# Linear attention beside a gated MLP: the key sum taken through DMAs and VectorE instead of one matmul, its den steps placed later, three loads joined

## The chip, the core and the metric

The program runs on one core of one Trainium2 chip. The metric is the device time of one execution in microseconds (us). The kernel before took 179.99 us (median of three runs, 179.78 to 180.3). Engines are named as in the profile: PE (TensorE), DVE (VectorE), ACT (ScalarE), POOL (GpSimd) and SP, which here only issues DMAs.

## What is computed

One input `x` (2048 tokens of 512 features, bfloat16) goes through two branches, mixed by a gate per token:

```python
phi = lambda t: jnp.where(t > 0, t + 1, jnp.exp(t)) + 1e-6
pq, pk = phi(q), phi(k)                     # q, k, v = x @ wqkv, 32 heads of 16
kv  = einsum("bhsd,bhse->bhde", pk, v)
z   = einsum("bhsd->bhd", pk)               # sum of phi(k) over all tokens
den = einsum("bhqd,bhd->bhq", pq, z)[..., None] + 1e-6
a   = (einsum("bhqd,bhde->bhqe", pq, kv) / den) merged @ wo
b   = (silu(x @ w1) * (x @ w3)) @ w2        # hidden width 1376
g   = sigmoid((x * gate_w).sum(-1))
out = g * a + (1 - g) * b
```

What the change touches is `z`: 512 sums over 2048 tokens, which every token's `den` needs, and so must be present in all 128 partitions.

## The kernel before, in words

Tokens are taken in 16 tiles of 128 (`t`), and in the second half in four blocks of 512 (`tb`). The order of the instructions on every engine is the order in which they are written in the program; each engine works through its own list in that order, and waits where an operand is not ready.

**First half.** Loads are issued on SP: `x` in natural layout (`xN`, L116 and L128), `x` transposed by DMA (`xT`, L110), and all weights (L113, L130 to L143). For each token tile PE projects q and k (L167); ACT takes the exponential and DVE the rest of phi (L180 to L185). PE accumulates `G = x^T phi(k)` in four PSUM banks (L215). POOL adds each tile of phi(k) into `zacc`, 128 partitions by 512 features (L195, L199); the last tile's sum is written as bfloat16 to `zaccb`. So `zaccb` still has to be summed over the 128 partitions.

**Between the halves.** One matmul of a matrix of ones by `zaccb` (L372) gives that sum in all partitions, and a DVE copy (L373) puts it in `zb`. Then `G` is copied out of PSUM to `Gsb` (L376 DVE, L378 ACT).

**Second half.** For block `tb`, `glu_step(tb, fc)` runs ten times (fc = 0..9): four matmuls with `w1` (L262), four with `w3` (L268), Silu on ACT (L273) and a product on DVE (L274) that writes `hT`. Both matmul groups use `mm_tile()`, four PSUM banks in turn: a group can start when the reader of the group four before it is done, and for the `w3` group that reader is the DVE product two chunks earlier. In block 0 other steps stand between the chunks: `den_step(0..3)` after chunks 0, 1, 3 and 6, `kv_step` after chunk 2 (L385, L389), `m2_step` after chunk 4 (L398 to L402), and `rem_step(0)` after chunk 7 (L229 to L252: the last 96 columns of the hidden width and the gate column, whose result is transposed by a DMA). `rem_step` takes two of the same four banks. Then four `out_step`s, one for each token tile: L410 multiplies `pqT` by `M2`, L423 multiplies `hT` by `w2`, L427 mixes them, L440 stores. The den steps of the next block are spread over them.

**A den step.** `den_products(t)` (POOL, L281) multiplies phi(q) of tile t by `zb` into `pr`; `den_sums(t)` (DVE) reduces it by head (L285), adds 1e-6 (L288) and takes the reciprocal (L292); `den_scale(t)` (POOL, L296) scales phi(q), and a transposing DMA on SP (L301) puts it into `pqT`, which L410 reads. `den_step(t)` issues the sums of t, the products of t + 1 and the scale of t, in that order; the products of tile 0 are issued once, ahead of the loop (L442).

Of the kernel before, what the change touches and what calls it, by code (L numbers as in the profile page):

```python
# [9 lines left out]
ALU = mybir.AluOpType  # L10
AX = mybir.AxisListType
FP32 = mybir.dt.float32
BF16 = mybir.dt.bfloat16
# [3 lines left out]
def kernel(  # L17
# [17 lines left out]
    nc = tc.nc  # L35
    P = nc.NUM_PARTITIONS

    Bb, S, D = A_x.shape
# [3 lines left out]
    KC = D // P  # L42
# [4 lines left out]
    FC = F // P  # L47
# [10 lines left out]
    w1_r = B_w1.rearrange("(kc d) f -> d kc f", d=P)  # L58
    w3_r = B_w3.rearrange("(kc d) f -> d kc f", d=P)

    consts = ctx.enter_context(tc.tile_pool(name="consts", bufs=1))
    work = ctx.enter_context(tc.tile_pool(name="work", bufs=2))
    psum = ctx.enter_context(tc.tile_pool(name="psum", bufs=1, space=bass.MemoryType.PSUM))
    ctx.enter_context(tc.manual_schedule())

    warm = nc.const_aps.tensor(1.0, [P, 256], BF16)
# [1 line left out]
    make_identity(nc, ident[:])  # L68


    ones = consts.tile([P, P], BF16, name="ones")
    nc.gpsimd.memset(ones[:], 1.0)
    bmask = consts.tile([P, HPC, Dh], BF16, name="bmask")
    nc.gpsimd.memset(bmask[:], 1.0)
    nc.gpsimd.affine_select(
        out=bmask[:], in_=bmask[:], pattern=[[-Dh, HPC], [0, Dh]], compare_op=ALU.is_ge,
# [3 lines left out]
        out=bmask[:], in_=bmask[:], pattern=[[Dh, HPC], [0, Dh]], compare_op=ALU.is_ge,  # L80
# [5 lines left out]
    zacc = consts.tile([P, D], FP32, name="zacc")  # L86
    zaccb = consts.tile([P, D], BF16, name="zaccb")
    zb = consts.tile([P, D], BF16, name="zb")

# [9 lines left out]
    w1 = consts.tile([P, KC, F0], BF16, name="w1")  # L101
    w3 = consts.tile([P, KC, F0], BF16, name="w3")
    w2 = consts.tile([P, FC + 1, D], BF16, name="w2")
    xT = consts.tile([P, KC, S], BF16, name="xT")
    act_pre = consts.tile([P, 1], BF16, name="act_pre")
    dq = nc.sync
# [5 lines left out]
    def load_wqk(kc):  # L112
        dq.dma_start(out=wqk[:, kc, :], in_=wqkv_r[:, kc, 0 : 2 * D])  # L113
# [6 lines left out]
    nc.scalar.dma_start(out=touch[:], in_=wqkv_r[:, 1:3, 0:16])  # L120
    for kc in range(KC):
        load_wqk(kc)
    natural = {3: (2, 4), 5: (4, 8), 7: (8, 12), 11: (12, 16)}
    for t in range(2, NT):
        load_xT(t)
        if t in natural:
# [2 lines left out]
    with nc.allow_non_contiguous_dma(reason="gate column"):  # L129
        dq.dma_start(  # L130
            out=wr[:, :, 2 * FR : NR], in_=gate_w.rearrange("(kc d o) -> d kc o", d=P, o=1)
        )
    dq.dma_start(out=wr[:, :, 0:FR], in_=w1_r[:, :, F0:F])
    dq.dma_start(out=wr[:, :, FR : 2 * FR], in_=w3_r[:, :, F0:F])
    for w, w_r, cuts in ((w1, w1_r, (0, KC)), (w3, w3_r, (0, 2, KC))):
        for a, b in zip(cuts, cuts[1:]):
            dq.dma_start(out=w[:, a:b, :], in_=w_r[:, a:b, 0:F0])
    dq.dma_start(out=wv[:], in_=wqkv_r[:, :, 2 * D : 3 * D])
    dq.dma_start(out=wo[:], in_=A_wo.rearrange("(kc d) n -> d kc n", d=P))
    w2_r = B_w2[0:F0, :].rearrange("(fc f) d -> f fc d", f=P)  # L140
    for a, b in ((0, 5), (5, FC)):
        dq.dma_start(out=w2[:, a:b, :], in_=w2_r[:, a:b, :])
    dq.dma_start(out=w2[:FR, FC, :], in_=B_w2[F0:F, :])  # L143

    pq = consts.tile([P, NT, D], BF16, name="pq")
# [11 lines left out]
    def mm_tile():  # L157
        turn["mm"] += 1
        return bank[4 + (turn["mm"] - 1) % 4]
# [53 lines left out]
    def g_step(t, kcs=range(KC)):  # L213
        for kc in kcs:
            nc.tensor.matmul(  # L215
                bank[kc][:], lhsT=xN[:, t, kc * P : (kc + 1) * P], rhs=pk[t][:],
                start=(t == 0), stop=(t == NT - 1),
            )


    def rem_step(tb):

        hr = hrem[tb % 2]
        for half in range(2):
            ps = mm_tile()[:].rearrange("p (j n) -> p j n", j=2)
            for j in range(2):
                t = tb * TPB + half * 2 + j
                for kc in range(KC):
                    nc.tensor.matmul(  # L229
                        ps[:, j, 0:NR], lhsT=xT[:, kc, t * P : (t + 1) * P],  # L230
                        rhs=wr[:, kc, 0:NR], start=(kc == 0), stop=(kc == KC - 1),
                    )
            t0 = tb * TPB + half * 2
            sg = work.tile([P, 2, FR], BF16, tag="sgr", name="sgr")
            nc.scalar.activation(out=sg[:], in_=ps[:, :, 0:FR], func=ACT.Silu)
            nc.scalar.activation(
                out=th_all[:, t0 : t0 + 2], in_=ps[:, :, 2 * FR], func=ACT.Tanh, scale=0.5
            )
            nc.vector.tensor_tensor(
                out=hr[:, half * 2 : half * 2 + 2, 0:FR], in0=ps[:, :, FR : 2 * FR],  # L240
                in1=sg[:], op=ALU.mult,
            )
        tl = slice(tb * TPB, (tb + 1) * TPB)
        nc.vector.tensor_scalar(
            out=g_all[:, tl], in0=th_all[:, tl], scalar1=0.5, scalar2=0.5,
            op0=ALU.mult, op1=ALU.add,
        )
        nc.vector.tensor_scalar(
            out=omg_all[:, tl], in0=th_all[:, tl], scalar1=-0.5, scalar2=0.5,
            op0=ALU.mult, op1=ALU.add,  # L250
        )
        dq.dma_start(  # L252
            out=hT[tb][:, FC, :].rearrange("p (tt q) -> p tt q", q=P),
            in_=hr[:].rearrange("p tt f -> p (tt f)"), transpose=True,
        )

    def glu_step(tb, fc):
        fs = slice(fc * P, (fc + 1) * P)
        tok = slice(tb * TB, (tb + 1) * TB)
        g_ps = mm_tile()  # L260
        for kc in range(KC):
            nc.tensor.matmul(  # L262
                g_ps[:], lhsT=w1[:, kc, fs], rhs=xT[:, kc, tok],
                start=(kc == 0), stop=(kc == KC - 1),
            )
        u_ps = mm_tile()
        for kc in range(KC):
            nc.tensor.matmul(  # L268
                u_ps[:], lhsT=w3[:, kc, fs], rhs=xT[:, kc, tok],
                start=(kc == 0), stop=(kc == KC - 1),  # L270
            )
        sg = work.tile([P, TB], BF16, tag="sg", bufs=3, name="sg")
        nc.scalar.activation(out=sg[:], in_=g_ps[:], func=ACT.Silu)  # L273
        nc.vector.tensor_tensor(out=hT[tb][:, fc, :], in0=u_ps[:], in1=sg[:], op=ALU.mult)  # L274
# [4 lines left out]
    def den_products(t):  # L279
        pr[t] = work.tile([P, D], FP32, tag="pr", bufs=3, name="pr")  # L280
        nc.gpsimd.tensor_tensor(out=pr[t][:], in0=pq[:, t, :], in1=zb[:], op=ALU.mult)  # L281
# [21 lines left out]
    def den_step(t):  # L303

        den_sums(t)
        if t + 1 < NT:
            den_products(t + 1)
        den_scale(t)
# [57 lines left out]
    for t in range(2, NT):  # L366
# [1 line left out]
        if t + 2 < NT:  # L368
            k_step(t + 2)
        g_step(t)  # L370
    z_ps = mm_tile()
    nc.tensor.matmul(z_ps[:], lhsT=ones[:], rhs=zaccb[:], start=True, stop=True)  # L372
    nc.vector.tensor_copy(out=zb[:], in_=z_ps[:])  # L373
    for kc in range(KC):
        if kc % 2 == 0:
            nc.vector.tensor_copy(out=Gsb[:, kc, :], in_=bank[kc][:])  # L376
# [3 lines left out]
    def kv_step():  # L380
        kv_ps = ab_tile()[:].rearrange("p (c q) -> p c q", q=P)
        for c in range(KC):
            cs = slice(c * P, (c + 1) * P)
            for kc in range(KC):
                nc.tensor.matmul(  # L385
                    kv_ps[:, c, :], lhsT=wv[:, kc, cs], rhs=Gsb[:, kc, cs],
                    start=(kc == 0), stop=(kc == KC - 1),
                )
        nc.vector.tensor_tensor(  # L389
            out=kvT[:], in0=kv_ps,  # L390
            in1=bmask[:].rearrange("p h d -> p (h d)")[:, None, :].to_broadcast([P, KC, P]),
            op=ALU.mult,
        )

    def m2_step():
        for c in range(KC):
            ps = ab_tile()
            nc.tensor.matmul(ps[:], lhsT=kvT[:, c, :], rhs=wo[:, c, :], start=True, stop=True)  # L398
            if c % 2 == 0:
                nc.scalar.activation(out=M2[:, c, :], in_=ps[:], func=ACT.Copy)  # L400
            else:
                nc.vector.tensor_copy(out=M2[:, c, :], in_=ps[:])  # L402
# [36 lines left out]
                cs = slice(2 * P, D)  # L439
            dq.dma_start(out=rows[:, cs], in_=o[:, cs])  # L440

    den_products(0)  # L442
    den_at = {0: 0, 1: 1, 3: 2, 6: 3}
    for tb in range(NTB):
        for fc in range(FC):
            glu_step(tb, fc)
            if tb == 0:
                if fc in den_at:
                    den_step(den_at[fc])
                if fc == 2:  # L450
                    kv_step()
                if fc == 4:
                    m2_step()
                if fc == 7:
                    rem_step(0)
        for tt in range(TPB):
            out_step(tb, tt)
            if tb + 1 < NTB:
                if tt == 0:
                    hT[tb + 1] = work.tile([P, FC + 1, TB], BF16, tag="hT", name="hT")  # L460
                if tt == 1:
                    rem_step(tb + 1)
                den_step((tb + 1) * TPB + tt)
# [30 lines left out]
```

## Time and profile before

| | |
|---|---|
| runs | 179.78, 179.99, 180.3 us |
| the profiled execution: its own time | 179.65 us |
| its span, first to last instruction | 177.8 us |
| PE busy | 174.2 us (98% of the span), 880 matmuls |
| DVE, ACT, POOL busy | 100.4, 62.3, 63.0 us |
| granted TensorE clock | 1.000 over the span |

The profile's page gives busy time by engine, groups of instructions by line, the DMA issues with their time to landing, and the chain of work that ended last. The timeline gives single instructions: start, duration, engine, line, tiles. A matmul of 128x512 is recorded with 379 ns, but four in a row take 0.86 us, since each starts before the one ahead of it has ended; the chain counts the pace, 0.216 us each.

### The profile page before, as it was taken

The numbers are of one execution on the slowest core, as the hardware profiler recorded it, in microseconds if no ns is written. First come the engines' busy times: TensorE is split into PE (matmuls) and PEld (weight loads), VectorE is DVE, ScalarE is ACT, GpSimd is POOL, SyncE is SP. The second block draws the span as 40 slices with busy tenths as digits, with TensorE's granted clock in tenths as the row PEclk, the third lists the DMA queues.
The fourth block names the chain that finished last, engine by engine and source line by source line (L and its number), as shares of the span: only waits on it lengthen the run. The fifth ranks groups of instructions, "written<-read, shape, count | busy, mean of one in ns | idle before, by whom it ended". The sixth has DMA issues, their size and how long they took to land.

```text
span 177.8 us, 2504 instructions
## 1 busy us (share of the span) xinstructions
PE 174.2 (98%) x880; PEld 84.1 (47%) x880; DVE 100.4 (56%) x194; ACT 62.3 (35%) x113; POOL 63.0 (35%) x105
## 2 busy tenths in 40 slices
PE   8999999999999999999999999999999999999993
PEld 5444444444454464644444464444445444444453
DVE  0299888888899662576344166634325564333222
ACT  3354544544735332331332223242321223342130
POOL 5086667656577340446300044540004432000000
PEclk9999999999999999999999999999999999999999
DMA  5989769994002111233100013520000342000001
GB/s 175 269 206 207 149 121 240 404 383 166 4 0 59 30 36 27 55 77 104 30 0 4 0 33 85 92 59 4 0 0 29 89 92 59 0 0 0 29 33 59
DMA packets 28940, 15.15 MB, mean 85 GB/s; under 512 B 20896, under 2 KB 27264, under 8 KB 28928
## 3 DMA queue, kind: packets, MB, share of 16 engines
q1 hardware_dynamic: 28656, 14.98, 31.9%
q8 instruction: 7, 0.11, 0.3%
q10 hardware_dynamic: 272, 0.01, 0.1%
q14 instruction: 5, 0.04, 0.1%
HBM read 8.43 MB, written 2.10 MB: 59 GB/s over the span
## 4 chain that ended last, share of the span: by engine, by line
PE 98%; DVE 0%; issue 0%
PE bank L423 21%; PE bank L262 19%; PE bank L268 19%; PE bank L167 16%; PE bank L215 8%; PE bank L410 8%; PE bank L229 3%; PE bank L315 2%; PE bank L385 1%; PE bank L398 0%; PE bank L322 0%; DVE o L427 0%; PE bank L372 0%
## 5 line engine op out<-in xcount | busy, mean ns | idle before, releaser
L274 DVE TENSOR_TENSOR hT<-bank,sg 128x512 bf16<-128x512 f32 x40 | 27.2, 680 | 30.9 <-PE bank L268 30.9
L268 PE MATMUL bank<-xT,w 128*128 128x512 bf16 x160 | 41.1, 379 | 0.0
L262 PE MATMUL bank<-xT,w 128*128 128x512 bf16 x160 | 41.1, 379 | 0.0
L423 PE MATMUL bank<-w,hT 128*128 128x512 bf16 (+3 forms) x198 | 40.7, 355 | 0.0
L273 ACT ACTIVATE sg<-bank 128x512 bf16<-128x512 f32 x40 | 23.9, 597 | 46.9 <-PE bank L262 46.9
L296 POOL TENSOR_TENSOR pqs<-pq,rden 128x512 bf16<-128x512 bf16 x16 | 16.9, 1055 | 65.0 <-issue 60.0
L167 PE MATMUL bank<-wqk,xT 128*128 128x512 bf16 x128 | 30.8, 383 | 0.0
L427 DVE SCALAR_TENSOR_TENSOR o<-bank,omg_all,aga 128x512 bf16<-128x512 f32 (+2 forms) x18 | 12.5, 692 | 28.1 <-PE bank L423 28.0
L423 PEld LDWEIGHTS <-hT 128*128 128x128 bf16 (+1 forms) x198 | 18.5, 98 | 19.8
L199 POOL TENSOR_TENSOR zacc<-zacc,pk 128x128 f32<-128x128 f32 x56 | 23.5, 449 | 10.8 <-DVE pk L185 10.8
L268 PEld LDWEIGHTS <-w 128*128 128x128 bf16 x160 | 15.7, 98 | 18.9
L262 PEld LDWEIGHTS <-w 128*128 128x128 bf16 x160 | 15.6, 98 | 18.4
L415 ACT ACTIVATE aga<-bank,g_all 128x512 f32<-128x512 f32 x16 | 11.0, 687 | 28.9 <-PE bank L410 28.9
L167 PEld LDWEIGHTS <-xT 128*128 128x128 bf16 x128 | 12.5, 99 | 15.5 <-issue 0.5
L281 POOL TENSOR_TENSOR pr<-pq,zb 128x512 f32<-128x512 bf16 x16 | 18.4, 1154 | 1.9 <-DVE zb L373 1.9
L215 PE MATMUL bank<-pk,xN 128*128 128x512 bf16 x64 | 16.5, 379 | 0.0
L410 PE MATMUL bank<-M,pqT 128*128 128x512 bf16 x64 | 16.4, 378 | 0.0
L180 ACT ACTIVATE eq<-bank 128x512 bf16<-128x512 f32 x16 | 9.4, 597 | 16.1 <-PE bank L167 16.1
L185 DVE SCALAR_TENSOR_TENSOR pk<-bank,emk 128x512 bf16<-128x512 f32 x16 | 11.1, 692 | 1.7
L180 ACT ACTIVATE ek<-bank 128x512 bf16<-128x512 f32 x16 | 9.4, 597 | 6.7 <-PE bank L167 6.7
L185 DVE SCALAR_TENSOR_TENSOR pq<-bank,emq 128x512 bf16<-128x512 f32 x16 | 11.1, 692 | 0.6
L285 DVE TENSOR_REDUCE den<-pr 128x32 f32<-128x512 f32 x16 | 10.8, 677 | 0.0
(47 smaller groups left out, 81.6 us busy)
## 6 DMA issues: line engine op xcount, KB each, us to landing
w<-in_B_w_dram SPq DMA_DIRECT2D x4, 640.0 KB, 9.6
out_dram<-o SPq DMA_DIRECT2D x15, 128.0 KB, 1.9
xN<-in_A_x_dram SPq DMA_DIRECT2D x3, 512.0 KB, 4.2
w<-in_B_w_dram SPq DMA_DIRECT2D x1, 1280.0 KB, 7.6
wqk<-in_A_wqkv_dram SPq DMA_DIRECT2D x4, 256.0 KB, 4.0
xN<-in_A_x_dram SPq DMA_DIRECT2D x2, 256.0 KB, 2.9
wv<-in_A_wqkv_dram SPq DMA_DIRECT2D x1, 512.0 KB, 10.8
wo<-in_A_wo_dram SPq DMA_DIRECT2D x1, 512.0 KB, 11.1
```

Source lines behind the costliest of these rows:

```text
L167: nc.tensor.matmul(ps[:], lhsT=xT[:, kc, t * P : (t + 1) * P], rhs=w[:, kc, :], start=(kc == 0), stop=(kc == KC - 1),)
L180: nc.scalar.activation(out=e[:], in_=ps[:], func=ACT.Exp)
L185: nc.vector.scalar_tensor_tensor(out=dst, in0=ps[:], scalar=0.0, in1=em[:], op0=ALU.max, op1=ALU.add)
L199: nc.gpsimd.tensor_tensor(out=(zaccb if t == NT - 1 else zacc)[:, cs], in0=zacc[:, cs], in1=pk[t][:, cs], op=ALU.add,)
L215: nc.tensor.matmul(bank[kc][:], lhsT=xN[:, t, kc * P : (kc + 1) * P], rhs=pk[t][:], start=(t == 0), stop=(t == NT - 1),)
L262: nc.tensor.matmul(g_ps[:], lhsT=w1[:, kc, fs], rhs=xT[:, kc, tok], start=(kc == 0), stop=(kc == KC - 1),)
L268: nc.tensor.matmul(u_ps[:], lhsT=w3[:, kc, fs], rhs=xT[:, kc, tok], start=(kc == 0), stop=(kc == KC - 1),)
L273: nc.scalar.activation(out=sg[:], in_=g_ps[:], func=ACT.Silu)
L274: nc.vector.tensor_tensor(out=hT[tb][:, fc, :], in0=u_ps[:], in1=sg[:], op=ALU.mult)
L281: nc.gpsimd.tensor_tensor(out=pr[t][:], in0=pq[:, t, :], in1=zb[:], op=ALU.mult)
L410: nc.tensor.matmul(a_ps[:], lhsT=pqT[:, c, ts], rhs=M2[:, c, :], start=(c == 0), stop=(c == KC - 1),)
L423: nc.tensor.matmul(b_ps[:, 0:w], lhsT=hT[tb][:n, fc, tl], rhs=w2[:n, fc, cs], start=(fc == 0), stop=(fc == FC),)
```

## The change

```diff
-    ones = consts.tile([P, P], BF16, name="ones")
-    nc.gpsimd.memset(ones[:], 1.0)
+    zaT = consts.tile([P, KC, P], BF16, name="zaT")
+    zTb = consts.tile([P, KC], BF16, name="zTb")
+    zrow = dram.tile([1, D], BF16, name="zrow")
...
-    natural = {3: (2, 4), 5: (4, 8), 7: (8, 12), 11: (12, 16)}
+    natural = {3: (2, 4), 5: (4, 8), 8: (8, 16)}
...
-    for w, w_r, cuts in ((w1, w1_r, (0, KC)), (w3, w3_r, (0, 2, KC))):
+    for w, w_r, cuts in ((w1, w1_r, (0, KC)), (w3, w3_r, (0, KC))):
...
-    for a, b in ((0, 5), (5, FC)):
-        dq.dma_start(out=w2[:, a:b, :], in_=w2_r[:, a:b, :])
+    dq.dma_start(out=w2[:, 0:FC, :], in_=w2_r)
...
-    z_ps = mm_tile()
-    nc.tensor.matmul(z_ps[:], lhsT=ones[:], rhs=zaccb[:], start=True, stop=True)
-    nc.vector.tensor_copy(out=zb[:], in_=z_ps[:])
+    dq.dma_start(out=zaT[:], in_=zaccb[:], transpose=True)
+
+    def z_step():
+        zT = work.tile([P, KC], FP32, tag="zT", bufs=1, name="zT")
+        nc.vector.tensor_reduce(out=zT[:], in_=zaT[:], op=ALU.add, axis=AX.X)
+        nc.vector.tensor_copy(out=zTb[:], in_=zT[:])
+        with nc.allow_non_contiguous_dma(reason="512 sums to one row"):
+            dq.dma_start(out=zrow[0, :].rearrange("(kc p) -> p kc", p=P), in_=zTb[:])
+        dq.dma_start(out=zb[:], in_=zrow[0:1, :].to_broadcast([P, D]))
...
-    den_products(0)
-    den_at = {0: 0, 1: 1, 3: 2, 6: 3}
+    den_at = {4: 0, 5: 1, 6: 2, 8: 3}
     for tb in range(NTB):
         for fc in range(FC):
             glu_step(tb, fc)
             if tb == 0:
+                if fc == 0:
+                    z_step()
+                    den_products(0)
                 if fc in den_at:
                     den_step(den_at[fc])
```

The sum over partitions is now made in five steps: a transposing DMA turns `zaccb` so that tokens lie along the free axis; DVE reduces each of the 512 rows to one number, and copies them to bfloat16; a DMA writes the 512 numbers as one row to a scratch tensor in DRAM; a second DMA reads that row into all 128 partitions of `zb`. The reduction, the copy and the last two DMAs are issued after chunk 0 of block 0, and `den_products(0)` after them. The den steps 0 to 3 move to after chunks 4, 5, 6 and 8. Three DMAs are added and three go, since three pairs of loads (`xN` tiles 8 to 15, `w3`, `w2`) become one DMA each; the two halves of `xN` are now issued together, after the transposing load of tile 8.

## The prediction

> **What bounds the kernel now.** I read four views, in this order. First the page's busy times and the chain that ended last: is one engine the whole time?
>
> ```profile
> PE 174.2 (98%) x880; PEld 84.1 (47%) x880; DVE 100.4 (56%) x194; ACT 62.3 (35%) x113; POOL 63.0 (35%) x105
> ...
> PE 98%; DVE 0%; issue 0%
> ```
>
> It is. TensorE's matmuls follow one another from 0.84 us to 175.07 us. Then the waits of PE alone, which hold one line:
>
> ```profile
> PE bank L315 <- PEq L478: 0.8, 1, 0.8
> ```
>
> PE waits only for the program's start. So nothing is gained by making another engine earlier; what counts is matmul work removed and waits of PE made new. Third, the chain in order of time, around the change:
>
> ```profile
> 45.89 0.86 PE bank L215 x4
> 46.75 0.22 PE bank L372
> 46.97 0.86 PE bank L262 x4
> ```
>
> The matmul that goes is 0.22 us of the chain (its pace of 0.216 us; the 379 ns of its row overlap its neighbour), with no gap on either side.
>
> Fourth, the timeline from 44 to 54 us, for what the den path costs on the engines beside PE:
>
> ```profile
> 44.70 1.63 POOL L199 TENSOR_TENSOR zaccb<-zacc,pk 128x128 bf16<-128x128 f32 x4 [0.69 <-DVE pk L185]
> ...
> 48.25 2.27 POOL L281 TENSOR_TENSOR pr<-pq,zb 128x512 f32<-128x512 bf16 x2 [1.92 <-DVE zb L373]
> ...
> 51.41 1.06 POOL L296 TENSOR_TENSOR pqs<-pq,rden 128x512 bf16<-128x512 bf16 x1 [0.89 <-DVE rden L292]
> ...
> 52.42 1.16 POOL L281 TENSOR_TENSOR pr<-pq,zb 128x512 f32<-128x512 bf16 x1
> 52.49 3.86 SPq L301 DMA_TRANSPOSE pqT<-pqs  x2
> 52.50 1.12 DVE L288 TENSOR_SCALAR den<-den 128x32 f32<-128x32 f32 x1
> ```
>
> The last line matters most: L288 takes 0.18 us in 15 of its 16 instances, but 1.12 us here, where it started 0.08 us after a POOL product and ended 0.04 us after it. I read that as DVE held until POOL's instruction was over. The reader should also see that `zb` was there by 48.25 us, when POOL's first product started.
>
> **Gain.** 1 matmul x 0.216 us = 0.22 us, 0.12% of the time, and no more than that. The DVE copy L373 (0.68 us) and POOL's memset (0.20 us) go too; both lie beside PE work, so they give nothing.
>
> **When zb arrives now.** `zaccb` is done at 44.70 + 1.63 = 46.33. SP is free (its last load was issued by 38.3 us) and issues the transposing DMA at once; the transposing DMAs of `pqT` land 2.4 us after issue, so `zaT` is there at 48.8. The DVE reduction stands behind chunk 0's product, which starts at 49.44 because ACT loads a table until 48.80; DVE's next step starts 0.6 us later, so the wait on `zaT` costs nothing. The reduction reads 512 elements per partition as L285 does: 0.68 us (pace 0.71), from 50.0 to 50.7; the copy of 128x4, as L288 or L248, 0.18 us. SP issues the row write at 50.93. DVE has time here, since the old den steps 0 and 1 are gone from this stretch.
>
> Two DMA latencies follow one after the other, and these decide the case. Call them a (column of 512 two-byte elements to DRAM) and b (one 1 KB row to 128 partitions). The nearest rows are:
>
> ```profile
> out_dram<-o SPq DMA_DIRECT2D x15, 128.0 KB, 1.9
> ...
> xN<-in_A_x_dram SPq DMA_DIRECT2D x2, 256.0 KB, 2.9
> ...
> pqT<-pqs SPq DMA_TRANSPOSE x16, 2.4
> ...
> wr<-in_gate_w_dram SPq DMA_DIRECT2D x1, 1.0 KB, 2.8
> ```
>
> For a: the gate column is the same 512 elements of 2 bytes in the other direction, 2.8 us; a store to DRAM takes 1.5 us at least and 3.7 us at most (the range of `out_dram`). I take 2.8, the row nearest in shape, with ends 1.5 and 3.7. For b: 128 rows of 1 KB, as `out_dram` (1.9), in a quiet queue; the quickest load of `xN` took 2.7 with twice the bytes. I take 2.0, ends 1.5 and 2.7. So a + b = 4.8, between 3.0 and 6.4, and with 0.1 us for two hand-overs POOL starts `den_products(0)` at 50.93 + 0.1 + 4.8 = 55.83.
>
> Two rules of the Trainium skill bear on a ("DMA: Bandwidth & Descriptors"). Its "Specifications" say that below 512 bytes a transfer is done as read-modify-write, which speaks against a: the gate row is a load and cannot show it. Its "Anatomy of one DMA" has a fixed cost of about 2.0 us plus bytes over 436 GB/s, by which (an estimate) a + b would be 4.3 us and the change would come out 0.03 us faster. No run here shows a two-byte store yet.
>
> **What waits behind it.** DVE meets `den_sums(0)` after chunk 4's product. Chunk 4's matmuls end at 56.49 - 0.22 = 56.27; its product runs from 56.37, the next DVE step can start at 56.96. `pr` of tile 0 is ready at 55.83 + 1.15 + 0.05 = 57.03: DVE stands for 0.07 us. Behind that wait on DVE are L288, L292, the two M2 copies and the products of chunks 5 to 9; PE waits for those products, through the bank that the `w3` group two chunks later (or a half of `rem_step`) takes.
>
> I now lay DVE's list out with start-to-start paces from the old timeline: product 0.59, L285 0.71, L288 0.22, L292 0.27, M2 copy 0.61; POOL's products 1.12 to 1.16; L296 starts 0.42 after L292 does and takes 1.01. (Laid out the same way, the old list comes within 0.1 us of its own timeline.) L285 of tile 0 at 57.03, L288 at 57.74. POOL's next product runs from 56.95 to 58.1, so L288 is held to 58.1, L292 at 58.17, M2 copies 58.45 and 59.05, chunk 5's product 59.66, then L285 to L292 of tile 1 (60.26 to 61.46), chunk 6's product 61.46, L285 of tile 2 62.05, L288 62.76. POOL scales tile 1 from 61.6 and multiplies tile 3 from 62.6 to 63.77: L288 is held again, for 0.9 us. L292 63.83, chunk 7's product 64.10 to 64.78.
>
> The old distances leave these due times for PE, 0.22 us earlier than before and 0.16 us earlier than the chain prints, since a matmul starts that much before its neighbour's end: chunk 7's `w3` group at 61.3 needs chunk 5's product, ended 60.3; the second half of `rem_step` at 62.83 needs chunk 6's, ended 62.1; chunk 8's `w3` group at 64.36 needs chunk 7's, ended 64.78 + 0.06. The last is late by 0.48 us. After it PE has its slack back: the later groups, `pqT` of tile 0 (landed 62.1, needed 67.4) and the transposed rest (landed 69.0, needed 70.6) are in time.
>
> So: -0.22 + 0.48 = **+0.26 us**. Generally, the stall is 0.19 us for a + b up to 4.5 (the hold on L288 alone), and grows one for one after that: change = max(-0.03, a + b - 4.54). If the hold did not happen, it would be -0.22.
>
> **The rest, at nothing.** SP: the row write and row read stand ahead of `pqT` of tiles 0 to 3 and the transposed rest, but those are not ready before 59.7, and the read is issued by 53.8. POOL: nothing but den work stands behind `den_products(0)`. Joined loads: the second half of `xN` puts 512 KB ahead of `xT` of tile 9; at the 2 us or so that 512 KB take (207 to 269 GB/s in those slices) tile 9 lands near 20 us, and PE needs it at 26. `w3` and `w2` are in before 44 us and used at 47 and 68; without that cover each would cost what it is late. Three DMAs go and three come, so the later ones keep their places in the program's rotation of DMA semaphores.
>
> **Rivals.** (1) Early zb: a = 2.3, b = 1.9 gives 4.2, hence -0.03; for it speaks the 1.5 us of the shortest store. (2) Late zb, ending slower: a two-byte store takes as long as the longest store, 3.7, and the broadcast 2.7. Then `pr` is ready at 58.6, DVE stands from 56.96 with M2 and five products behind it, and PE stalls at chunk 7, at `rem_step` and at chunk 8: +1.9 us. It decides from a + b = 5.1 (+0.54 us, 0.3%). Against it: the queue is quiet at that time (0 GB/s from 44 to 47 us). (3) A joined load is late and PE waits in the first half: the six microseconds of slack speak against it. (4) Faster by over 0.3% would need 0.54 us, more than twice the one matmul; only an effect that this profile does not show could do it.
>
> **How the numbers follow.** 0.3% of the time, 0.54 us, is about what a measurement of this kernel can tell from no change. Against the profiled execution's 179.65 the sum gives 179.91; the median of the runs lies 0.34 higher, so I forecast 180.25. Chances: the forecast's case (a + b from 4.5 to 5.1, 0 to +0.54) 0.34; early (1) 0.16; late (2) 0.44, as a two-byte store to DRAM is in no row; joined loads (3) 0.02; (4) 0.04. So faster 0.04, same 0.50, slower 0.46. The range goes from -0.4 (the matmul gone, no stall, and the spread of the runs) to +1.8 (nearly both upper ends): 179.6 to 181.8.
>
> **What would show it.** In the new profile: the first POOL product near 55.8; DVE's wait ahead of the first L285 below 0.2 us; two L288 (tiles 0 and 2) lengthened by POOL; one wait of PE at chunk 8's `w3` group, released by chunk 7's product, near 0.5 us; PE's last matmul about 0.3 us later. Wrong: the row write takes over 3.5 us, then PE's waits begin at chunk 7; or PE waits anywhere before 47 us.

## The result, and the profile after

The changed kernel took **195.28 us** (median of seven runs, 193.83 to 195.83) against 179.99 for the kernel before in the same comparison; the ratio is 1.0846, 95% interval 1.0824 to 1.0868. The forecast was 180.25, with 181.8 as the upper end. The profiled execution took 193.83 us, its span is 192.1: 14.2 and 14.3 us more than the profiled execution before. It is the quickest of the seven; what the others have above it, about 1 us, no trace here shows. Line numbers in the changed kernel and in the experiments are a few higher than in the kernel before: its L268, the `w3` group, is L269 below.

The page of the changed kernel, busy time and the chain that ended last (shares of the span by engine):

```profile
PE 175.9 (92%) x879; PEld 85.0 (44%) x879; DVE 100.5 (52%) x195; ACT 62.3 (32%) x113; POOL 62.8 (33%) x104
...
PEclk9999999999999655999999999999999999999999
...
PE 83%; DMA 10%; DVE 2%; ACT 2%; POOL 1%; issue 0%
```

DMAs are now a tenth of the chain, where PE had 98% of it, and three of the 40 slices have a granted clock of 0.5 to 0.6 (the digits of PEclk are tenths). The waits of PE alone, in us in total, times, longest:

```profile
PE bank L269 <- DVE hT L275: 12.6, 1, 12.6
```

Beside the 0.8 us of the program's start it is a single wait, of a `w3` group for a product of DVE. What DVE itself waited for, the same view for that engine:

```profile
DVE den L286 <- POOL pr L282: 13.7, 1, 13.7
```

And the timeline between (start, duration, engine, line; SPq is the issue of a DMA on SP):

```profile
46.42 1.21 SPq L374 DMA_TRANSPOSE zaT<-zaccb  x1
...
50.11 0.68 DVE L378 TENSOR_REDUCE zT<-zaT 128x4 f32<-128x512 bf16 x1
...
51.02 0.38 SPq L381 DMA_DIRECT2D zrow<-zTb  x1
...
66.14 0.34 SPq L382 DMA_DIRECT2D zb<-zrow  x1
69.67 2.26 POOL L282 TENSOR_TENSOR pr<-pq,zb 128x512 f32<-128x512 bf16 x2 [23.28 <-DMA zb<-zrow]
70.85 0.69 DVE L286 TENSOR_REDUCE den<-pr 128x32 f32<-128x512 f32 x1 [13.71 <-POOL pr L282]
...
72.27 1.22 DVE L412 CAST M<-bank 128x512 bf16<-128x512 f32 x2
...
73.41 0.68 DVE L275 TENSOR_TENSOR hT<-bank,sg 128x512 bf16<-128x512 f32 x1
...
74.14 1.86 PE L269 MATMUL bank<-xT,w 128*128 128x512 bf16 x4 [12.62 <-DVE hT L275]
```

Read it downwards. The transposing DMA, the reduction and the issue of the row write stand within 0.1 us of where the prediction put them. Then 15 us pass between the issue of the write (51.02) and the issue of the read that waits for it (66.14). DVE stands at `den_sums(0)` with two M2 copies and chunk 5's product behind it, and chunk 7's `w3` group on PE waits for that product. The DMA issues of the page say the same (KB, us to landing):

```profile
zb<-zrow SPq DMA_DIRECT2D x1, 128.0 KB, 3.5
...
zaT<-zaccb SPq DMA_TRANSPOSE x1, 2.4
zrow<-zTb SPq DMA_DIRECT2D x1, 1.0 KB, 15.1
```

Of the 14.3 us of span, 12.6 are the wait. Another 1.8 pass at a granted clock of 0.5: the four matmuls after the wait take 1.86 us in place of 0.86, and the 16 of `rem_step` 2.14 in place of 1.33. The matmul that went gives 0.2 back. How much of the 1.8 a full clock would save is another question (experiment 4).

### The profile page after: what moved, and what is told of

It reads as the page before. It is cut to its first block, busy times and chain, and to the rows that moved or that the text cites. A ratio compares the mean times of both kernels' runs of the same rounds, so it can differ in the third digit from the quotient of the medians.

```text
span 192.1 us, 2504 instructions
## 1 busy us (share of the span) xinstructions
PE 175.9 (92%) x879; PEld 85.0 (44%) x879; DVE 100.5 (52%) x195; ACT 62.3 (32%) x113; POOL 62.8 (33%) x104
## 4 chain that ended last, share of the span: by engine, by line
PE 83%; DMA 10%; DVE 2%; ACT 2%; POOL 1%; issue 0%
PE bank L433 20%; PE bank L269 15%; PE bank L168 15%; PE bank L263 14%; DMA zrow<-zTb 8%; PE bank L420 7%; PE bank L216 7%; PE bank L230 3%; DMA zb<-zrow 2%; PE bank L316 2%; DVE hT L275 1%; ACT L274 1%; DVE M L412 1%; POOL pr L282 1%; ACT Gsb L388 1%; PE bank L323 0%
## 5 line engine op out<-in xcount | busy, mean ns | idle before, releaser
L269 PE MATMUL bank<-xT,w 128*128 128x512 bf16 x160 | 41.9, 385 | 12.6 <-DVE hT L275 12.6
L433 PE MATMUL bank<-w,hT 128*128 128x512 bf16 (+3 forms) x198 | 40.7, 356 | 0.0
L297 POOL TENSOR_TENSOR pqs<-pq,rden 128x512 bf16<-128x512 bf16 x16 | 16.9, 1055 | 57.9 <-issue 53.2
L269 PEld LDWEIGHTS <-w 128*128 128x128 bf16 x160 | 15.8, 99 | 32.0 <-issue 13.4
L433 PEld LDWEIGHTS <-hT 128*128 128x128 bf16 (+1 forms) x198 | 18.5, 98 | 19.9
L437 DVE SCALAR_TENSOR_TENSOR o<-bank,omg_all,aga 128x512 bf16<-128x512 f32 (+2 forms) x18 | 12.5, 692 | 28.1 <-PE bank L433 28.0
L168 PEld LDWEIGHTS <-xT 128*128 128x128 bf16 x128 | 12.6, 99 | 15.5 <-issue 0.6
L286 DVE TENSOR_REDUCE den<-pr 128x32 f32<-128x512 f32 x16 | 10.8, 677 | 13.7 <-POOL pr L282 13.7
L420 PE MATMUL bank<-M,pqT 128*128 128x512 bf16 x64 | 16.4, 378 | 0.0
```

The source lines that it names most:

```text
L168: nc.tensor.matmul(ps[:], lhsT=xT[:, kc, t * P : (t + 1) * P], rhs=w[:, kc, :], start=(kc == 0), stop=(kc == KC - 1),)
L269: nc.tensor.matmul(u_ps[:], lhsT=w3[:, kc, fs], rhs=xT[:, kc, tok], start=(kc == 0), stop=(kc == KC - 1),)
L420: nc.tensor.matmul(a_ps[:], lhsT=pqT[:, c, ts], rhs=M2[:, c, :], start=(c == 0), stop=(c == KC - 1),)
L433: nc.tensor.matmul(b_ps[:, 0:w], lhsT=hT[tb][:n, fc, tl], rhs=w2[:n, fc, cs], start=(fc == 0), stop=(fc == FC),)
```

## The experiments

Two questions: what makes the store take 15 us, and does everything lost come from it?

**1. Nine DMAs one at a time.** To the kernel before, a tail was added after the last instruction; each DMA waits for the one ahead of it. `ready` is a DVE copy into the source, which waits for the store before it. The stores take a 128x4 tile whose content does not matter; `d_b` has 512 rows of 32 elements and `d_c` 512 rows of 256, of which the first element is written:

```diff
+        ready(src2)
+        dq.dma_start(out=d_a[0, :].rearrange("(kc p) -> p kc", p=P), in_=src2[:])
...
+        dq.dma_start(out=d_b[:, 0].rearrange("(kc p) -> p kc", p=P), in_=src2[:])
...
+        dq.dma_start(out=d_c[:, 0].rearrange("(kc p) -> p kc", p=P), in_=src2[:])
...
+        dq.dma_start(out=d_d[0, :].rearrange("(p kc) -> p kc", p=P), in_=src2[:])
...
+        dq.dma_start(out=row[:], in_=x2d[0:1, :].to_broadcast([P, D]))
...
+        dq.dma_start(out=row[:], in_=x2d[0:P, :])
```

> The kernel before, and after its last instruction nine DMAs one at a time (each waits for the one before through a DVE copy into its source or out of its target), so the whole time grows and is not compared: only the times to landing are read. Stores of a 128x4 bfloat16 tile: a) 512 pieces of 2 bytes to 1 KB in a row, as the change has it; b) 512 pieces of 2 bytes, 64 bytes apart; c) 512 pieces of 2 bytes, 512 bytes apart; d) 128 pieces of 8 bytes to 1 KB in a row; f) 128 pieces of 2 bytes to 256 bytes in a row; e) 512 pieces of 4 bytes to 2 KB in a row; reads: one 1 KB row of DRAM by all 128 partitions, then 128 different rows; then a) again. Theory 1, every small write costs the same wherever it goes (13.8 us after the last of 512 packets = 27 ns each): a 15, b 15, c 15, d 4.8, f 4.8, e 15 us. Theory 2, small writes wait for one another only inside one short stretch of DRAM: a 15, b and c near 2.5, e about 7.5, d about 4.8, f about 15 if stretches are served side by side and 4.8 if not. Theory 3, the 15 us were a thing of the place in the kernel and not of the store: a near 2.8, as the gate column's load. Reads: 3.5 us for the one row if reading the same row costs, and 1.9 for 128 different rows; both alike if not.

The DMA issues of this run, in KB and us to landing:

```profile
d_a<-src SPq DMA_DIRECT2D x1, 1.0 KB, 13.9
d_b<-src SPq DMA_DIRECT2D x1, 1.0 KB, 2.4
d_c<-src SPq DMA_DIRECT2D x1, 1.0 KB, 1.8
d_d<-src SPq DMA_DIRECT2D x1, 1.0 KB, 3.0
d_f<-src SPq DMA_DIRECT2D x1, 0.2 KB, 16.6
d_e<-src SPq DMA_DIRECT2D x1, 2.0 KB, 10.3
d_g<-src SPq DMA_DIRECT2D x1, 1.0 KB, 14.3
```

Theory 3 falls: in an empty queue the store takes 13.9 and 14.3 us. Theory 1 falls: the same 512 pieces of 2 bytes, 64 bytes apart, land in 2.4 us. Number and size of the pieces are the same there, so what counts is how close together they lie. Pieces of 8 bytes side by side (`d_d`) take 3.0 us, pieces of 4 bytes (`d_e`) 10.3: the fewer fall into a stretch, the quicker. And 128 pieces in 256 bytes (`d_f`, 16.6 us) are no quicker than 512 in 1 KB, as theory 2 has it if different stretches are served side by side. The reads: the two `row` loads took 2.0 and 2.8 us (smallest and largest of the tile's landings); the timeline has the one row read by all partitions as the slower.

**2. The matmul put back, the rest of the change kept.**

```diff
-    dq.dma_start(out=zaT[:], in_=zaccb[:], transpose=True)
...
+    z_ps = mm_tile()
+    nc.tensor.matmul(z_ps[:], lhsT=ones[:], rhs=zaccb[:], start=True, stop=True)
+    nc.vector.tensor_copy(out=zb[:], in_=z_ps[:])
...
-                    z_step()
```

> The matmul of ones and its copy to zb put back, everything else of the change kept (den steps after chunks 4, 5, 6, 8, three loads joined). Theory 1, the whole loss is the DMA route: 180.0 to 180.3 us, with at most one stall of 0.2 us at chunk 8 where POOL holds DVE's L288. Rival, the moved den steps or the joined loads cost part of it: over 181 us, with a wait of PE in the first half or at chunks 5 to 9.

179.80 us, ratio to before 0.9995 (0.9967 to 1.0024). This is 0.2 us under the expected range. So the joined loads and the moved den steps cost nothing that these runs can tell (the interval is -0.6 to +0.4 us of 15.3); the loss is the DMA route. The stall that the prediction's schedule had for an early `zb` is there too, in the timeline of this run:

```profile
62.86 1.15 POOL L281 TENSOR_TENSOR pr<-pq,zb 128x512 f32<-128x512 bf16 x1
62.93 1.11 DVE L288 TENSOR_SCALAR den<-den 128x32 f32<-128x32 f32 x1
...
64.08 0.35 DVE L292 RECIPROCAL rden<-den 128x32 f32<-128x32 f32 x1
...
64.35 0.63 DVE L274 TENSOR_TENSOR hT<-bank,sg 128x512 bf16<-128x512 f32 x1
```

L288 again ends with POOL's product; chunk 8's `w3` group then takes 0.97 us of the chain in place of 0.86, a stall of 0.11 (0.19 in my formula).

**3. Pieces of 8 bytes.** Each partition writes its four sums side by side; the products read `zb` with a stride.

```diff
-            dq.dma_start(out=zrow[0, :].rearrange("(kc p) -> p kc", p=P), in_=zTb[:])
+            dq.dma_start(out=zrow[0, :].rearrange("(p kc) -> p kc", p=P), in_=zTb[:])
...
+            in1=zb[:].rearrange("p (q c) -> p c q", c=KC), op=ALU.mult,
```

> The changed kernel, with the 512 sums written in the order (partition, chunk), so that 128 pieces of 8 bytes go to the same 1 KB; zb is read in that order and the products take it with a stride. Theory 1, the number of writes sets the store: landing 1.3 + 128 x 0.027 = 4.8 us, read 3.5, a + b = 8.3, change by the formula +3.7 less whatever the clock adds: 183 to 184.5 us. Rival, the bytes or the stretch of DRAM set it: the landing stays at 15 us and the time at 195. If a store of 128 pieces were as quick as the full rows of out (1.9), 180.9.

182.31 us, ratio 1.0117 (1.0059 to 1.0174), quicker than theory 1 had it, and far from its rival's 195. The landings:

```profile
zb<-zrow SPq DMA_DIRECT2D x1, 128.0 KB, 4.3
...
zrow<-zTb SPq DMA_DIRECT2D x1, 1.0 KB, 2.6
```

a + b is 6.9, and the prediction's formula, a + b - 4.54, gives +2.4 us; measured +2.5. The same 1 KB of DRAM in a quarter of the pieces costs 12.5 us less. Theory 1, a fixed price for each write, had 4.8 us for this store and falls here too.

**4. PE kept busy through the wait.** 56 matmuls, whose result nobody reads, stand in front of the group that waits.

```diff
...
+        if tb == 0 and fc == 7:
+            keep_busy(56)
         u_ps = mm_tile()
```

> The changed kernel, with 56 idle matmuls of 128x512 (56 x 0.216 = 12.1 us, into a bank whose content has been read) ahead of chunk 7's w3 group, where PE waits 12.6 us. Theory 1: part of the loss is the TensorE clock, granted at 0.5 after the long wait (four matmuls took 1.86 us in place of 0.86, the rem step 2.14 in place of 1.33, together 1.8 us). With PE busy the clock stays at 1.00 and the time falls by 1.5 to 1.8 us to 193.5 to 193.8. Rival, the clock costs nothing that the wait had not cost already (the next stalls at rem_step and chunk 8, 1.4 us by my schedule, come instead): 195.0 to 195.3.

194.35 us, ratio to before 1.0784 (1.0713 to 1.0855). The interval holds the changed kernel's 1.0846, and the four runs, 193.56 to 195.22, reach from theory 1's range to the rival's: the times do not decide between the two. The traces say more. The granted clock is 1.00 throughout, so the 1.8 us are gone, but PE now waits where the slow clock had hidden it. This run's waits of PE:

```profile
PE bank L277 <- DVE hT L283: 1.6, 2, 1.0
```

0.67 us are left of the long wait, and 0.98 are chunk 8's group waiting for chunk 7's product, the stall that follows when the prediction's list of DVE is laid out for a late `zb` (1.1 us). In the chain of this run, chunk 7's and chunk 8's `w3` groups:

```profile
74.14 1.04 PE bank L277 x4
...
78.55 1.02 PE bank L277 x4
```

And chunk 8's group in the chain of the changed kernel, where chunk 7's started at 74.14 too:

```profile
79.00 0.86 PE bank L269 x4
```

It ends at 79.57 in place of 79.86, 0.3 us earlier, and the spans are 191.8 and 192.1 us. So in these two executions the slow clock made instructions 1.8 us longer, but cost only 0.3: the rest would have been lost to the wait for chunk 7's product. That is near the rival.

**5. Nine more stores.** The same tail with the distance of the pieces as the variable, and one (`near`) with the pieces side by side but in another order. In gap1, as in the change, the 32 pieces that lie in the same 64 bytes come from 32 neighbouring partitions, one from each; in `near` they come from 8, four from each.

```diff
+        for n in (1, 2, 4, 8, 16, 32):
+            d = dram.tile([D, n], BF16, name=f"gap{n}")
+            ready()
+            dq.dma_start(out=d[:, 0].rearrange("(kc p) -> p kc", p=P), in_=src2[:])
...
+        d = dram.tile([1, D], BF16, name="near")
+        dq.dma_start(out=d[0, :].rearrange("(p kc) -> p kc", p=P), in_=src8[:, :, 0])
```

> The kernel before with a second tail of single stores, each waiting for the one before; only times to landing are read. 512 pieces of 2 bytes with a distance of 2, 4, 8, 16, 32 and 64 bytes between them (gap1 to gap32), so that 32, 16, 8, 4, 2 and 1 of them fall into the same 64 bytes; then 512 pieces of 2 bytes side by side in the order (partition, chunk), so that 32 pieces that lie in the same 64 bytes come from neighbouring partitions and not from partitions far apart (near); then 128 pieces of 2 bytes 8 bytes apart (one); then 4 neighbouring elements of one partition (four). Theory A, what counts is how many pieces fall into one stretch: near about 14 us as gap1, and gap1 14, gap2 about 10, gap4 about 4 to 6, gap8 and wider near 2.5. Theory B, what counts is that different DMA engines write into one stretch at once: near well under gap1, 3 to 5 us. Both: one near 3 (8 pieces in 64 bytes), four near 1.8.

The timeline of DVE: each copy waits (in brackets, us) for the store before it, gap1 to gap32 first.

```profile
190.75 0.17 DVE L470 COPY src<-zb 128x4 bf16<-128x4 bf16 x1 [15.23 <-DMA gap<-src]
199.84 0.17 DVE L470 COPY src<-zb 128x4 bf16<-128x4 bf16 x1 [8.93 <-DMA gap<-src]
204.44 0.17 DVE L470 COPY src<-zb 128x4 bf16<-128x4 bf16 x1 [4.43 <-DMA gap<-src]
207.61 0.17 DVE L470 COPY src<-zb 128x4 bf16<-128x4 bf16 x1 [3.00 <-DMA gap<-src]
209.85 0.17 DVE L470 COPY src<-zb 128x4 bf16<-128x4 bf16 x1 [2.07 <-DMA gap<-src]
212.06 0.17 DVE L470 COPY src<-zb 128x4 bf16<-128x4 bf16 x1 [2.03 <-DMA gap<-src]
...
227.50 0.17 DVE L481 COPY src<-zb 128x4 bf16<-128x4 bf16 x1 [15.06 <-DMA near<-src]
...
231.08 0.17 DVE L470 COPY src<-zb 128x4 bf16<-128x4 bf16 x1 [3.21 <-DMA one<-src]
232.40 0.17 DVE L470 COPY src<-zb 128x4 bf16<-128x4 bf16 x1 [1.15 <-DMA four<-src]
```

Theory A fits: with 32, 16, 8, 4, 2 and 1 pieces in the same 64 bytes the waits are 15.2, 8.9, 4.4, 3.0, 2.1 and 2.0 us, `one` (8 pieces) is near its 3 with 3.2, and `four` with 1.15 is quicker than its 1.8. Theory B as it was put falls, since `near` takes as long as gap1; which DMA engine sends which piece no view shows, so the engines' part is tested only as far as 8 partitions in place of 32 go.

How long the stretch is these runs do not show. Doubling the distance halves the pieces in a stretch of 64 bytes, but just so in one of another length. It is hardly over 256 bytes, since `d_f` of experiment 1 fills no more and takes as long as the 1 KB of `d_a`. Of the last three distances little can be read: the same store, 64 bytes apart, made DVE wait 2.03 us here and 2.54 in experiment 1.

**6. No DRAM at all.** DVE writes each sum 128 times into a tile, and a second transposing DMA turns this into `zb`.

```diff
-        nc.vector.tensor_copy(out=zTb[:], in_=zT[:])
-        with nc.allow_non_contiguous_dma(reason="512 sums to one row"):
-            dq.dma_start(out=zrow[0, :].rearrange("(kc p) -> p kc", p=P), in_=zTb[:])
-        dq.dma_start(out=zb[:], in_=zrow[0:1, :].to_broadcast([P, D]))
+        nc.vector.tensor_copy(
+            out=zW[:].rearrange("p (c j) -> p c j", j=P),
+            in_=zT[:, :, None].to_broadcast([P, KC, P]),
+        )
+        dq.dma_start(
+            out=zb[:].rearrange("p (c q) -> p c q", q=P), in_=zW[:], transpose=True
+        )
```

> The changed kernel without DRAM: the DVE copy of the sums writes each of them 128 times into a 128x512 tile, and a second transposing DMA turns it into zb directly (a + b becomes one DMA of 2.4 us and a copy longer by some 0.5 us). zb at 54, before DVE asks for it. My formula: change -0.03 us, one stall near 0.2 us at chunk 8 from the hold of L288: span 177.7 to 177.9, time 179.6 to 180.1. Rival: a second transposing DMA, or a wider copy, costs PE something elsewhere: over 180.5.

179.75 us, ratio 1.0001 (0.9987 to 1.0015): no difference from before that the runs can tell, as the formula had it for an early `zb` (-0.03 us). The copy took 0.43 us, the DMA landed in 2.4, and POOL's first product started at 54.19.

**7. The same, with the den steps after chunks 3, 5, 7 and 8.**

```diff
-    den_at = {4: 0, 5: 1, 6: 2, 8: 3}
+    den_at = {3: 0, 5: 1, 7: 2, 8: 3}
```

> As the kernel with two transposes, but den steps 0 to 3 after chunks 3, 5, 7 and 8, where my schedule finds no late DVE product: PE without any wait, -0.22 us: span 177.6, time 179.5 to 180.0. Rival: a hold of L288 elsewhere makes a stall of 0.2 us or more, span as before or longer.

179.61 us, ratio 0.9986 (0.9973 to 0.9998). PE has no wait for DVE in the second half, and in the chain the first `out_step` starts at 67.08 us where the kernel before has 67.32: what remains is the gain of the one matmul. By the runs it is 0.14%, with an interval from 0.02 to 0.27%, so the times alone would hardly show it.

**8. The two-byte store kept, all four den steps after chunk 9.**

```diff
-    den_at = {4: 0, 5: 1, 6: 2, 8: 3}
...
-                if fc in den_at:
-                    den_step(den_at[fc])
+                if fc == FC - 1:
+                    for i in range(TPB):
+                        den_step(i)
```

> The changed kernel, two-byte store kept, with den steps 0 to 3 all after chunk 9, so that no DVE product of block 0 stands behind the wait for zb. Theory: PE runs on to the first out_step, due at 67.1, and waits there for pqT of tile 0: zb 69.6, product, sums, scale and transposing DMA end near 76, so a wait of 8.8 us in place of 12.6, a clock cost of 1 to 2 us at most, and no stalls after it at chunk 8: +9 to +11 us, 189 to 191. Rival, DVE's queue did not matter and PE waits for the store all the same: 195.

191.80 us, ratio 1.0650 (1.0629 to 1.0671), 0.8 us above the expected range. PE's long wait is now this:

```profile
PE bank L420 <- DMA pqT<-pqs: 9.2, 1, 9.2
```

So DVE's queue did matter: with no product of block 0 behind the wait, 12.6 us become 9.2. The clock takes back more than the 1 to 2 us that I had said, about 3: the first `out_step` runs at 0.5 (in the chain its 4 matmuls of L420 take 1.89 us in place of 0.86, its 11 of L433 4.41 in place of 2.38). Most of the loss stays, since the first `out_step` needs `pqT`, and `pqT` needs `zb`.

## Why the prediction was wrong, point by point

- **What bounds the kernel, and the gain (0.22 us):** right. The chain of experiment 7 has just this gain, once nothing new is late.
- **When zb arrives, up to the row write:** right; issue forecast at 50.93, seen at 51.02.
- **a, the row write:** this step failed. I took 2.8 us from the gate column, with 3.7 as the upper end; it took 15.1. The gate column is a load: its small pieces are reads of DRAM and writes of SBUF. I had named this difference, and put it into the chances, but not into the range; the rows used as bounds were stores in pieces of 1 KB. No row showed small pieces written side by side into DRAM, and so the upper end had no ground. The Trainium skill ("DMA: Bandwidth & Descriptors", "Specifications") says that below 512 bytes a transfer is a read-modify-write. That fits an order in which pieces of the same stretch must wait for one another; that this is the mechanism the runs do not show. Being small is not enough: 512 pieces of 2 bytes that lay 64 bytes apart landed in 2.4 us. The prediction's estimate from "Anatomy of one DMA", 4.3 us for a + b, fails likewise against the measured 18.6. That section gives its fixed cost for DMAs issued by GpSimd, and these are issued on SP.
- **b, the row read:** 3.5 us, where I had 2.0, ends 1.5 and 2.7. Outside too, by a smaller amount: 0.8 above the end.
- **What waits behind it:** right in its mechanism and in its rate. DVE stands at the sums of tile 0 (13.7 us), and PE waits first at chunk 7's `w3` group, as in rival (2). With the measured a + b = 18.6 the formula gives +14.0 us, and the profiled execution has +14.2 (the medians differ by 15.3). The parts agree less than the sum: laid out for so late a `zb`, my list has 1.4 us of stalls at `rem_step` and chunk 8 beside the long wait, which did not come because the clock stood at 0.5 and made the matmuls 1.8 us longer. The prediction had no clock in it; that the sum is so close is partly luck, as two amounts of like size stood in for each other. Experiment 4, with the full clock, has 0.98 us of the stalls at chunk 8, and experiment 3 has +2.5 against +2.4.
- **The hold of L288:** seen in the changed kernel (L289, 1.11 us in place of 0.18, beside POOL's product, and, as forecast, a shorter one at tile 0, 0.39 us) and in experiments 2 and 4 (1.11 us each; L297 in experiment 4). In experiment 7 all 16 took 0.18 us.
- **The rest at nothing:** right as far as experiment 2 can tell.
- **Chances:** late `zb` had 0.44, but the range was cut at its supposed upper end. Had the upper end stayed open, the price of one for one from a + b = 4.54 would have made any longer store plain.

## What to carry to other kernels

When a step is replaced by a chain of DMAs, look for a row with the same direction and the same piece size, and leave the upper end open if there is none; a load's time is no bound for a store. Small results that must be spread over partitions may be better kept off DRAM: a second transposing DMA did it here in 2.4 us, where the store and read took 18.6. If they must go there, write them in larger pieces: 8 bytes from each partition made it 6.9. And a wait put into an in-order engine costs what stands behind it: the same late `zb` cost 12.6 us of waiting with the products of block 0 behind it, and 9.2 without.

## What the runs showed of the hardware that was not expected

The 512 pieces were all sent within 0.4 us (51.9 to 52.3 in the trace of packets); the store's semaphore, which tells the waiting engine that the data has landed, rose 13.8 us later, and the DMA engines show a busy share of 0.00 meanwhile. So a DMA can be long with nothing to see in the busy share. In experiment 5 the wait for such a store went from 2.0 to 15.2 us by the distance of the pieces alone.

The clock: stretches of the changed kernel, with time, busy of each engine, granted clock, DMA share and GB/s.

```profile
62.40:63.40 1.00, 0.00 (x0) 0.00 (x0) 0.00 (x0) 0.00 (x0) 0.00 (x0) 1.00 0.00 0
63.40:64.40 1.00, 0.00 (x0) 0.00 (x0) 0.00 (x0) 0.00 (x0) 0.00 (x0) 0.74 0.00 0
64.40:65.40 1.00, 0.00 (x0) 0.00 (x0) 0.00 (x0) 0.00 (x0) 0.00 (x0) 0.50 0.00 0
...
77.00:78.00 1.00, 1.00 (x11) 0.97 (x10) 0.97 (x3) 0.39 (x2) 0.53 (x1) 0.73 0.37 75
78.00:79.00 1.00, 1.00 (x7) 0.46 (x5) 1.00 (x4) 0.39 (x2) 0.97 (x1) 1.00 0.28 56
```

PE stopped at 61.5 and the clock fell to 0.5 between 63.4 and 64.4; PE started at 74.14 and had the full clock again between 77 and 78. In experiment 8 PE stopped at 67.55 and started at 76.76, and both changes took longer:

```profile
67.00:70.00 3.00, 0.55 (x3) 0.06 (x1) 0.69 (x1) 0.32 (x1) 0.00 (x0) 1.00 0.27 73
...
72.00:74.00 2.00, 0.00 (x0) 0.00 (x0) 1.90 (x5) 0.00 (x0) 1.49 (x2) 0.60 0.00 0
...
81.00:83.00 2.00, 2.00 (x7) 0.80 (x6) 0.00 (x0) 0.00 (x0) 0.74 (x1) 0.59 0.32 66
```

If the clock steps once in such a stretch, between 1.00 and 0.50, the mean gives the moment: down 2.4 us after PE stopped in the changed kernel and 4.9 in experiment 8, up 3.4 and 5.9 us after it started. The Trainium skill ("TensorE: Matmul & The Clock Gate", "Part 1: The HAM clock gate") gives about 3.4 us of idle or busy time for a change. One of the four changes here agrees with that; the other three lie up to 2.5 us off it.

Open: by what mechanism small pieces that lie close together delay a store, and in how long a stretch; and why reading the one fresh row by all partitions took 3.5 to 4.3 us in the kernels, and 2.8 us at most for a row of the input (experiment 1).
